# Splitting a mix by head set and key half, and a 64x64-quadrant product with v in three parts, in an attention and feed-forward kernel

## The chip, the core and the metric

The kernel runs on one core of a Trainium2 chip. The metric is the device time of one execution in microseconds (us); lower is better. Names of engines are those of the profile: PE is the matrix engine and PEld its weight loads, DVE, ACT and POOL are the vector, scalar and general engines, SP issues nearly all DMAs.

## What is computed

The reference has two stages, in fp32. The first is attention in which the 12 heads are mixed twice, once before the softmax and once after it; the second is a feed-forward layer with a rational function between its two products.

```python
# q, k, v: (4, 12, 448, 64)
scores = scale * np.matmul(q, k.transpose(0, 1, 3, 2))
scores = np.einsum('bhij,hg->bgij', scores, w_pre)       # first mix
scores = scores - np.max(scores, axis=-1, keepdims=True)
attn = np.exp(scores)
attn = attn / (np.sum(attn, axis=-1, keepdims=True) + 1e-09)
attn = np.einsum('bhij,hg->bgij', attn, w_post)          # second mix
attn_out = np.matmul(attn, v)
...
h = x @ w_in                                             # x: (1792, 768)
P = a[0] + a[1] * h + a[2] * h * h + a[3] * h * h * h
Q = 1.0 + np.abs(b[0]) * np.abs(h) + np.abs(b[1]) * h * h
out = (P / (Q + 1e-6)) @ w_out                           # w_in: (768, 2048)
```

## The kernel before

**Attention.** The 448 query rows of each of the 4 batches are cut into four tiles T of up to 120 rows: 12 tiles have 120 rows, 4 have 88 (computed as 90). For a tile, `put_qk` makes the scores of one head pair at a time (L473, six of them a tile, four matmuls in the four 64x64 quadrants of PE), copies them to SBUF (tile `st`) and sends them by DMA into `d`, where the partitions are (query, head). A *group* is two blocks of 10 queries: six groups in a tile of 120 rows, four and a half in one of 88. `put_pre` does the first mix of a group (L540, four matmuls of 448 columns in the quadrants, into two PSUM banks of pool `ps_t`); DVE takes the row maximum (L547), ACT the exponential with its sum (L556), POOL and DVE the reciprocal, POOL scales the second mix's weights by it (tile `krs`, L576). Two groups later (`LAG`), `put_post` does the second mix (L617): 32 matmuls of 112 columns a group, each in a 64x32 piece of the array, into the two banks of pool `ps_a`. The four 32-row strips of a bank hold the four key quarters, and a block's 224 columns hold the two sets of six heads one behind the other. DVE transposes each bank in 32x32 blocks into `aa` (L633), where keys lie on partitions. When a tile's six groups are transposed, `put_av` multiplies with v (L676): for each half hv of the heads, 24 matmuls of 120 (90) columns, with 128 partitions of contraction, of which 112 carry keys and the rest zeros in v. One half fills one bank of `ps_t`. ACT copies the sum, rounded, to `xs` (L236), DVE writes the rest (L690), and DMAs store both parts to DRAM.

PSUM has eight banks of 128 x 512 words: two in pool `ps_s` (scores), four in `ps_t` (first mix and product with v), two in `ps_a`.

**Feed-forward.** 64 units (`put_unit`): 18 matmuls for h (L832), the rational function on ACT, DVE and POOL, 18 matmuls for the output (L921). Weights come as 64-bit numbers and are converted in pieces by ACT, POOL and DVE (`put_w`, L387 to L431): 16 pieces during attention, to DRAM and back, 48 in the second stage.

**What sets the order.** Nothing is ordered by hand. Each `put_` function adds operations with an engine, an estimated duration, what they depend on and a due time; `Plan.run` plays them through and emits the instructions in that order, engine by engine. On PE the operations of attention are chained (`pe`), each may start only after the one added before it. The duration is also where a mode ("quarters", "eighths", "columns") is named: PE pays `DRAIN` in the plan where the mode changes. Due times follow `tau`, which steps by `SLOT` for a group and `HALF` for half a group. The plan is built once, on the host; on the chip each engine takes its instructions in the given order and waits for what it needs. A `Ring` stands for the buffers of a pool: `take` gives the next, and it is free when the uses of the one n places before are done.

Of the kernel before, what the change touches and what calls it, by code (L numbers as in the profile page):

```python
# [21 lines left out]
G5 = 5  # L22
# [4 lines left out]
TI = 120  # L27
TQ = 128
NT = 4 * B
NJ, JT = 4, 112  # L30
NB, BT = 7, 32
G6 = H // 2
# [209 lines left out]
def mixed_attention_then_rational_ffn(ctx: ExitStack, tc, q, k, v, w, wmix, mask, a, b2, out):  # L242
# [14 lines left out]
          for n, i in (("s", 2), ("t", 4), ("a", 2))}  # L257
# [5 lines left out]
    def open_pools(stack, side, sizes):  # L263
# [9 lines left out]
        ("co", 2), ("ps_s", 2), ("ps_t", 4), ("ps_a", 2), ("a", 2), ("v", 2), ("xs", 1), ("xo", 2),  # L273
# [16 lines left out]
    SLOT, HALF = 3.85, 2.3  # L290
# [233 lines left out]
    def put_pre(g):  # L524
# [54 lines left out]
        slots = [R["ps_t"].take() for _ in range(nt)]  # L579
# [4 lines left out]
        for r in range(nt):  # L584
            o2 = add("dve", dve(S), top(r), [o, free[r]], at=at + 0.5 * r, after=prev[:])
            o3 = add("act", 0.84, exp(r), [o2], at=at + 0.5 * r, after=os[-1:])
            R["ps_t"].uses[slots[r].k].append(o3)
            os.append(o3)
            exps.append(o3)
            prev = [o2]  # L590
# [8 lines left out]
    def put_post(g, at):  # L599
# [37 lines left out]
        o5 = pe(0.95, post, o4 + slots, at, 0.1, "eighths")  # L637
# [12 lines left out]
    def put_v(b, at, gap=8.0):  # L650
        def load(j):
            def fn():
                if j == 0:
                    V[b] = sb["v"].tile([128, NJ, H, D], F32, tag="v", name="vv")
                nc.sync.dma_start(out=V[b][:, j], in_=v[b, :, j])
# [4 lines left out]
        for j in range(NJ):  # L660
            v_ld[b].append(bulk(0.63, load(j), [free] + v_ld[b][:1], at=at + gap * j, nbytes=128 * H * D * 4, since=at + gap * j))

    Xs = {}

    def put_av(T, hv, at):

        b, n, r, c0 = T // 4, rows[T], real[T], row0[T]
        box = {}

        def mm():  # L670
            t = bank("t")
            for pr in range(3):
                for j in range(NJ):
# [7 lines left out]
            box["t"] = t[:, 0:3 * n].rearrange("p (r w) -> p r w", r=3)[:, :, 0:r]  # L681

        def hi(eng):
            if hv == 0 and T % 4 == 0:
                Xs[b] = sb["xs"].tile([128, 2, 2, 3, S], F32R, tag="xs", name="xs")
            move(nc, eng, Xs[b][:, hv, 0, :, c0:c0 + r], box["t"])

        def lo():
            x = Xs[b][:, hv, :, :, c0:c0 + r]
            nc.vector.tensor_sub(x[:, 1], box["t"], x[:, 0].bitcast(F32))  # L690

        def store(hl, cols):
# [3 lines left out]

        slot = R["ps_t"].take()
        o = pe(24 * 0.108 * n / TI, mm, [evac[T], v_ld[b], slot], at, 0.2, "columns")
        av_op[T, hv] = o
        deps, after = [o], []  # L700
        if hv == 0 and T % 4 == 0:
            deps.append(R["xs"].take())
        else:
            after.append(xs_op[b][0])
        h_ = add(copies(3 * n, False, on=ON["x_hi"]), 0, hi, deps, at=at, after=after)
        l_ = add("dve", dve(3 * n), lo, [h_], at=at)
        xs_op.setdefault(b, []).append(h_)
        x_done.setdefault((b, hv), []).append(l_)
        R["ps_t"].uses[slot.k].append(l_)
        R["a"].uses[T].append(o)  # L710
        R["v"].uses[b].append(o)
        if T % 4 > 1:
            last = T % 4 == 3
            cols, done = (slice(c0, S), x_done[b, hv][3:]) if last else (slice(0, c0 + r), x_done[b, hv][:])
            for hl in range(2):
                when = at + (3.0 if last else 5.0) + (1.6 if last else 4.0) * (2 * hl + hv)
                o = bulk(0.45, store(hl, cols), done, at=when, nbytes=128 * 3 * max(cols.stop - cols.start, 240) * 4, late=1.0, since=when - 1.0)
                x_st.setdefault(b, []).append(o)
                R["xs"].uses[b].append(o)
# [12 lines left out]
    for pr in range(H // 2):  # L732
        put_qk(0, pr, at=-8.0 + pr, ps_="stat"[pr % 4])
    early, late = {}, {}
    for T in range(1, NT):
# [4 lines left out]
        for i, pr in zip((2, 3, 4) if T == 1 else (0, 2, 4, 5, 6) if n == 6 else (0, 1, 2, 3, 4), range(ahead, H // 2)):  # L740
            (late if i % 2 else early).setdefault(first[T - 1] + i // 2, []).append((T, pr))
    avs = {}
    for T in range(NT):
        for hv in range(2):
            avs.setdefault(first[T + 1] - 1 + LAG + 1 + hv, []).append((T, hv))
    for g in range(-1, len(groups) + LAG + 3):
# [315 lines left out]
```

## Time and profile before

| what | value |
|---|---|
| runs shown | 877.32, 881.3, 882.75 us (median 881.3) |
| the profiled execution | 876.83 us, of which 875.0 us from its first to its last instruction |
| attention, up to the first matmul of the feed-forward stage | 0 to 392.3 us of the span |
| feed-forward stage | 392.3 to 875.0 us |
| PE busy | 826.2 us, 94% of the span |
| DVE, ACT, POOL busy | 693.0, 483.8, 352.7 us |
| matmul records | 11,088, two for each fp32 matmul of attention |

A busy PE has a matmul somewhere in the array; it is not an array that is full. In attention several matmuls run beside each other in different pieces of the array, so what an operation costs is read from its start to the start of the next one, and not from the duration of its records.

### The profile page before, as it was taken

To read this page: it belongs to the slowest core of one execution; us is meant where nothing else is said; L and a number is where in the kernel's file an instruction comes from. 1 tells how busy PE (TensorE), PEld (TensorE's weight loads), DVE (VectorE), ACT (ScalarE), POOL (GpSimd) and SP (SyncE) were. 2 spreads that over 40 slices of the span, in tenths; PEclk is the share of its full clock that TensorE was granted. 3 is DMA by queue.
4 is the path that set the end of the run, shared out by engine and by line. 5 is a ranking of instruction groups with operands and counts; after the bars stand their busy time and mean duration, and the time that the engine had idled before them with its cause. 6 is when DMAs were issued, how large, how long until landed. Compare 5 with 4: busy or idle time off the path is not lost.

```text
span 875.0 us, 27000 instructions
## 1 busy us (share of the span) xinstructions
PE 826.2 (94%) x11088; PEld 641.3 (73%) x11088; DVE 693.0 (79%) x1279; ACT 483.8 (55%) x1057; POOL 352.7 (40%) x476
## 2 busy tenths in 40 slices
PE   5699989999999899989999999999999999999996
PEld 1255545555555555678898898999999999999995
DVE  5587868797888787847889999999899898666664
ACT  2355656555565554426666566755665567445641
POOL 2234434534344342313545554655555554112111
PEclk9899999999999999999999999999999999999999
DMA  6677788768767863399263337654556653256314
GB/s 204 196 214 216 235 250 239 220 213 283 226 219 232 277 206 117 96 333 372 75 222 121 101 121 265 216 194 138 178 211 208 259 171 126 73 202 231 127 64 147
DMA packets 77548, 170.64 MB, mean 195 GB/s; under 512 B 13072, under 2 KB 54384, under 8 KB 76272
## 3 DMA queue, kind: packets, MB, share of 16 engines
q1 hardware_dynamic: 76824, 167.95, 59.2%
q8 instruction: 87, 1.43, 0.7%
q10 hardware_dynamic: 600, 0.97, 0.3%
q14 instruction: 37, 0.30, 0.1%
HBM read 90.86 MB, written 39.32 MB: 149 GB/s over the span
## 4 chain that ended last, share of the span: by engine, by line
PE 62%; DVE 14%; DMA 5%; issue 4%; ACT 2%; POOL 1%; SPq 0%; DVEq 0%; ACTq 0%; POOLq 0%
PE ps_s L832 19%; PE ps_t L921 13%; PE ps_a L921 7%; PE ps_t L676 7%; PE ps_a L617 6%; PE ps_t L540 5%; PE ps_s L473 5%; DMA d<-st 2%; DVE cg L406 2%; DVE rc L877 1%; DMA x_scr<-xs 1%; DVE cm L412 1%; DVE sq L865 1%; DVE rc L881 1%; DVE sq L874 1%
## 5 line engine op out<-in xcount | busy, mean ns | idle before, releaser
L921 PE MATMUL ps_t<-g,w 128*128 128x448 f32 x768 | 177.4, 366 | 0.9 <-POOL g L891 0.9
L921 PEld LDWEIGHTS ps_t<-g,w 128*128 128x128 f32 x768 | 144.0, 188 | 13.7 <-POOL g L891 1.7
L617 PEld LDWEIGHTS ps_a<-e,krs 64*32 64x32 f32 x5760 | 77.9, 106 | 83.1 <-issue 47.1
L556 ACT ACTIVATE e<-ps_t,nm 128x448 f32<-128x448 f32 x180 | 112.8, 634 | 42.6 <-DVE nm L547 37.1
L891 POOL TENSOR_TENSOR g<-rc,g 128x448 fp32r<-128x448 f32 x55 | 69.1, 1256 | 159.8 <-ACT g L236 88.5
L832 PE MATMUL ps_s<-x,w 128*128 128x448 f32 x576 | 122.5, 366 | 2.1 <-DVE m L861 2.1
L633 DVE STREAM_TRANSPOSE aa<-ps_a 128x448 f32<-128x448 f32 (+1 forms) x184 | 107.8, 618 | 20.8 <-PE ps_a L617 20.1
L832 PE MATMUL ps_s<-xs,w 128*128 128x448 f32 x576 | 122.5, 366 | 1.5 <-DVE m L861 1.5
L397 POOL TENSOR_SCALAR cm<-cm 128x384 f32<-128x384 f32 x64 | 99.5, 1560 | 58.7 <-ACT cm L392 58.6
L617 PE MATMUL ps_a<-e,krs 64*32 64x112 f32 x5760 | 105.5, 263 | 13.1 <-issue 9.5
L832 PEld LDWEIGHTS ps_s<-x,w 128*128 128x128 f32 x576 | 108.0, 188 | 11.7 <-DVE m L861 2.8
L832 PEld LDWEIGHTS ps_s<-xs,w 128*128 128x128 f32 x576 | 107.8, 188 | 11.6 <-DVE m L861 2.6
L473 PE MATMUL ps_s<-kk,q 64*64 64x448 f32 x720 | 98.5, 559 | 15.5 <-DMA q<-in_q 5.3
L547 DVE TENSOR_REDUCE nm<-ps_t 128x1 f32<-128x448 f32 x180 | 104.5, 607 | 7.3 <-PE ps_t L540 6.1
L576 POOL TENSOR_SCALAR krs<-kpost,rr 128x64 f32<-128x64 f32 x180 | 80.3, 461 | 69.5 <-DVE rr L567 55.0
L540 PE MATMUL ps_t<-d,kpre 64*64 64x448 f32 x720 | 93.4, 560 | 7.1 <-DMA x_scr<-xs 2.1
L921 PE MATMUL ps_a<-g,w 128*128 128x448 f32 x384 | 96.5, 366 | 0.0
L236 ACT COPY st<-ps_s 120x448 f32<-120x448 f32 (+1 forms) x101 | 51.3, 533 | 71.8 <-PE ps_s L473 37.3
L676 PE MATMUL ps_t<-aa,vv 128*64 128x120 f32 (+1 forms) x1536 | 84.9, 266 | 0.9 <-DVE aa L633 0.8
L428 POOL TENSOR_TENSOR w<-cm,w 128x384 fp32r<-128x384 f32 x48 | 60.1, 1252 | 57.7 <-ACT w L236 55.8
L845 ACT ACTIVATE m<-ps_s,a_sb 128x448 f32<-128x448 f32 x64 | 46.1, 720 | 67.3 <-PE ps_s L832 67.2
L676 PEld LDWEIGHTS ps_t<-aa,vv 128*64 128x64 f32 x1536 | 77.5, 138 | 6.7 <-issue 5.1
(60 smaller groups left out, 1070.3 us busy)
## 6 DMA issues: line engine op xcount, KB each, us to landing
d<-st SPq DMA_DIRECT2D x144, 210.0 KB
cr<-in_w SPq DMA_DIRECT2D x64, 384.0 KB
o_scr<-o SPq DMA_DIRECT2D x36, 448.0 KB
o<-o_scr SPq DMA_DIRECT2D x36, 448.0 KB
x<-x_scr SPq DMA_DIRECT2D x5, 2688.0 KB
xs<-x_scr SPq DMA_DIRECT2D x4, 2688.0 KB
d<-st SPq DMA_DIRECT2D x42, 157.5 KB
x_scr<-xs SPq DMA_DIRECT2D x12, 540.0 KB
```

Of the source, the lines that this page charges most:

```text
L397: nc.gpsimd.tensor_scalar(out=m, in0=m, scalar1=F64_MIN, scalar2=F64_MAX, op0=ALU.max, op1=ALU.min)
L473: nc.tensor.matmul(box["s"][hh][i0:i1, 0:S], lhsT=Q[T][d, pr, i0:i1], rhs=K[b][d, pr, :], start=True, stop=True)
L540: nc.tensor.matmul(box[r if nt == 2 else 0]["t"][64 * c:64 * c + 64, 0:S], lhsT=kpre[p], rhs=Dt[T][p, kb + c if nt == 2 else kb, :], start ...
L547: nc.vector.tensor_reduce(out=nm, in_=box[r]["t"][:, 0:S], axis=AX.X, op=ALU.max, negate=True)
L556: nc.scalar.activation(e, box[r]["t"][:, 0:S], AF.Exp, bias=box[r]["nm"], accum_out=box[0]["sm"][:, r:r + 1])
L576: eng.tensor_scalar_mul(box[r]["kr"], kpost, rr)
L617: nc.tensor.matmul(banks[c]["p"][BT * q_:BT * (q_ + 1), j0:j0 + JT], lhsT=box[r]["kr"][p, m_, :], rhs=box[r]["e"][p, q_ * JT:(q_ + 1) * JT ...
L633: nc.vector.transpose(o, src)
L676: nc.tensor.matmul(t[64 * hf:64 * hf + 64, pr * n:(pr + 1) * n], lhsT=V[b][:, j, g, :], rhs=A[T][:, 3 * (g // G6) + j, 0:n // G5, G5 * (g ...
L832: nc.tensor.matmul(h[:, 0:S], lhsT=W[fi][:, wi, kk * 128:(kk + 1) * 128], rhs=x[:, kk // 3, xj, kk % 3, :], start=(n == 0), stop=(n == 3 * ...
L891: eng.tensor_sub(g[:, 1, :], box["rc"], g[:, 0, :].bitcast(F32))
L921: nc.tensor.matmul(O[key][:, 0:S], lhsT=W[fi][:, wi, DM + m * 128:DM + (m + 1) * 128], rhs=box["g"][:, gi, :], start=(f == 0 and n == 0), ...
```

## The change

**Second mix.** `put_post` now runs over the two key halves jh and the two head sets m_. A matmul covers 224 keys, so a group has 16 matmuls of 224 columns (32 records) where there were 32 of 112 (64 records). The strips of a bank hold (head set, key half), and its columns are keys alone.

**Product with v.** After the transposes, partitions 0 to 63 hold the first six heads and 64 to 127 the others, with all 448 keys in seven steps of 64 and no padding. v is laid out to match (a batch's four loads of 384 KB become three of 384 KB and one of 192 KB). `put_av` takes a head pair `pr` of each set at a time: 28 matmuls in the four 64x64 quadrants (head set by rows, parity of the head by columns), each head set into a bank of its own. There are three such parts a tile, in three consecutive groups, and the two banks are held over all three; the two evacuations (L236, then L699 in the new numbering) follow the third. The parts carry the mode "quarters", as the scores and the first mix do.

**Banks.** `ps_t` with four banks becomes `ps_t` and `ps_u` with two each. A group's first mix takes a pair. A table made ahead (`pairs`, `holds`) alternates the pairs; while one pair is held by the product with v, the first mixes of these groups all use the other.

**Plan.** `SLOT` goes from 3.85 to 3.65, `HALF` from 2.3 to 2.2, the duration given for the second mix from 0.95 to 0.77.

```diff
-    SLOT, HALF = 3.85, 2.3
+    SLOT, HALF = 3.65, 2.2
...
+        pair = pairs[g]
...
-                box[r]["t"] = bank("t")
+                box[r]["t"] = bank(pair)
...
             for r in range(nt):
-                for m_ in range(2):
-                    for q_ in range(NJ):
+                for jh in range(2):
+                    for m_ in range(2):
                         for c in range(2):
-                            p = slice(64 * c, 64 * c + 64)
-                            j0 = (2 * r + m_) * JT
+                            p, q_ = slice(64 * c, 64 * c + 64), BT * (2 * m_ + jh)
                             nc.tensor.matmul(
-                                banks[c]["p"][BT * q_:BT * (q_ + 1), j0:j0 + JT], lhsT=box[r]["kr"][p, m_, :],
-                                rhs=box[r]["e"][p, q_ * JT:(q_ + 1) * JT], start=True, stop=True)
+                                banks[c]["p"][q_:q_ + BT, JH * r:JH * (r + 1)], lhsT=box[r]["kr"][p, m_, :],
+                                rhs=box[r]["e"][p, JH * jh:JH * (jh + 1)], start=True, stop=True)
...
-        o5 = pe(0.95, post, o4 + slots, at, 0.1, "eighths")
+        o5 = pe(0.77, post, o4 + slots, at, 0.1, "eighths")
...
-    def put_av(T, hv, at):
+    def put_av(T, pr, at):
...
-        box = {}
+        if pr == 0:
+            sums[T] = {}, [R["ps_" + holds[T]].take() for _ in range(2)]
+        box, slots = sums[T]
...
-            t = bank("t")
-            for pr in range(3):
-                for j in range(NJ):
+            if pr == 0:
+                box.update(enumerate([bank(holds[T]), bank(holds[T])]))
+            for j in range(NB):
+                for hv in range(2):
                     for hf in range(2):
-                        g = 2 * (3 * hv + pr) + hf
+                        p, g = slice(64 * hv, 64 * hv + 64), 2 * pr + hf
                         nc.tensor.matmul(
-                            t[64 * hf:64 * hf + 64, pr * n:(pr + 1) * n],
-                            lhsT=V[b][:, j, g, :],
-                            rhs=A[T][:, 3 * (g // G6) + j, 0:n // G5, G5 * (g % G6):G5 * (g % G6 + 1)],
-                            start=(j == 0), stop=(j == NJ - 1))
+                            box[hv][64 * hf:64 * hf + 64, pr * n:(pr + 1) * n], lhsT=V[b][p, j, g, :],
+                            rhs=A[T][p, j, 0:n // G5, G5 * g:G5 * (g + 1)],
+                            start=(j == 0), stop=(j == NB - 1))
...
-        o = pe(24 * 0.108 * n / TI, mm, [evac[T], v_ld[b], slot], at, 0.2, "columns")
+        o = pe(14 * 0.107 * n / TI, mm, [evac[T], v_ld[b]] + (slots if pr == 0 else []), at, 0.2, "quarters")
...
+    pairs, holds, other = {}, {}, {"t": "u", "u": "t"}
+    for g in range(len(groups) + LAG + 4):
+        now, kept = avs.get(g, ()), avs.get(g - 1, ())
+        pairs[g] = pairs[g - 1] if any(pr for _, pr in now) or kept and kept[0][1] == 2 else other[pairs.get(g - 1, "t")]
+        for T, pr in now:
+            if pr == 0:
+                holds[T] = other[pairs[g]]
```

On PE, the stretch of the program in which the product with v of the second tile stands, before. `aa,vv` is the product with v, `e,krs` the second mix, `d,kpre` the first mix, `kk,q` the scores; a row's last figure is the number of matmuls.

```order
L617 MATMUL ps_a<-e,krs 32x112 x32
L676 MATMUL ps_t<-aa,vv 64x120 x24
L473 MATMUL ps_s<-kk,q 64x448 x4
L540 MATMUL ps_t<-d,kpre 64x448 x4
L473 MATMUL ps_s<-kk,q 64x448 x4
L617 MATMUL ps_a<-e,krs 32x112 x32
L676 MATMUL ps_t<-aa,vv 64x120 x24
L540 MATMUL ps_t<-d,kpre 64x448 x4
L617 MATMUL ps_a<-e,krs 32x112 x32
L540 MATMUL ps_t<-d,kpre 64x448 x4
```

The same stretch on PE in the changed kernel; L681 is the product with v, L541 the first mix.

```order
L617 MATMUL ps_a<-e,krs 32x224 x16
L681 MATMUL ps_t<-aa,vv 64x120 x28
L541 MATMUL ps_u<-d,kpre 64x448 x4
L473 MATMUL ps_s<-kk,q 64x448 x4
L617 MATMUL ps_a<-e,krs 32x224 x16
L681 MATMUL ps_t<-aa,vv 64x120 x28
L541 MATMUL ps_u<-d,kpre 64x448 x4
L617 MATMUL ps_a<-e,krs 32x224 x16
L681 MATMUL ps_t<-aa,vv 64x120 x28
L541 MATMUL ps_u<-d,kpre 64x448 x4
L473 MATMUL ps_s<-kk,q 64x448 x4
```

Where two products stood, three stand, each behind a second mix and ahead of a first mix, and the first mixes in between all go to pair `ps_u`, the last two of them with one second mix and one part between.

On DVE, the evacuations of the same tile's products before: one piece each, eight rows apart.

```order
L690 TENSOR_TENSOR xs<-ps_t,xs 128x3x120
L238 COPY st<-ps_s 120x448
L547 TENSOR_REDUCE nm<-ps_t 128x1 x2
L238 COPY st<-ps_s 120x448 x2
L633 STREAM_TRANSPOSE aa<-ps_a 128x2x7x32
L567 RECIPROCAL rr<-sm 128x2
L633 STREAM_TRANSPOSE aa<-ps_a 128x2x7x32
L690 TENSOR_TENSOR xs<-ps_t,xs 128x3x120
```

And on DVE in the changed kernel, such a place.

```order
L633 STREAM_TRANSPOSE aa<-ps_a 128x2x7x32 x2
L568 RECIPROCAL rr<-sm 128x2
L699 TENSOR_TENSOR xs<-ps_t,xs 128x3x120 x2
L548 TENSOR_REDUCE nm<-ps_u 128x1 x2
L238 COPY st<-ps_s 120x448
```

Both evacuations now stand behind the third part, in a row, ahead of the next row maxima.

Over the whole program DVE has 101 copies of scores to `st` (L238) where it had 86, ACT 91 where it had 106. At the end of attention, the last products were 48 matmuls of 90 columns in a row (two halves) and are 84 (three parts), with the feed-forward stage's first matmuls right behind.

## Rows read from the trace of the kernel before

**Rows 1.** The page, part 1: busy time, share of span, instructions.

```profile
PE 826.2 (94%) x11088; PEld 641.3 (73%) x11088; DVE 693.0 (79%) x1279; ACT 483.8 (55%) x1057; POOL 352.7 (40%) x476
```

**Rows 2.** Stages: window, length, busy PE, PEld, DVE, ACT, POOL, clock, DMA, GB/s.

```profile
49.40:372.10 322.70, 305.21 (x7821) 181.82 (x7818) 256.27 (x551) 178.63 (x483) 132.92 (x282) 1.00 0.72 217
392.30:875.00 482.70, 470.49 (x2307) 431.90 (x2304) 397.87 (x655) 284.78 (x525) 203.89 (x151) 1.00 0.51 174
108.00:130.00 22.00, 17.53 (x457) 9.80 (x450) 14.82 (x33) 12.02 (x33) 6.86 (x17) 1.00 0.85 252
262.00:284.00 22.00, 21.96 (x509) 12.47 (x506) 19.64 (x43) 12.41 (x34) 10.87 (x22) 1.00 0.75 230
```

**Rows 3.** What PE waited for, 20 to 392 us: total us, times, longest.

```profile
PE ps_a L617 <- issue: 9.5, 10, 2.0
PE ps_s L473 <- DMA q<-in_q: 5.3, 1, 5.3
PE ps_a L617 <- DVE aa L633: 2.6, 4, 0.8
PE ps_t L540 <- DMA x_scr<-xs: 2.1, 1, 2.1
```

**Rows 4.** PE's timeline, 42 to 60 us: start, length.

```profile
43.49 1.08 PE L617 MATMUL ps_a<-e,krs 64*32 64x112 f32 x64
44.49 0.98 PE L540 MATMUL ps_t<-d,kpre 64*64 64x448 f32 x8
45.30 0.93 PE L473 MATMUL ps_s<-kk,q 64*64 64x448 f32 x8
46.16 0.61 PE L617 MATMUL ps_a<-e,krs 64*32 64x112 f32 x32
46.70 0.98 PE L540 MATMUL ps_t<-d,kpre 64*64 64x448 f32 x8
...
49.37 2.12 PE L676 MATMUL ps_t<-aa,vv 128*64 128x90 f32 x48
51.43 0.98 PE L473 MATMUL ps_s<-kk,q 64*64 64x448 f32 x8
```

**Rows 5.** PE's timeline, 370 to 376 us: a product with v of 120 rows.

```profile
372.05 2.75 PE L676 MATMUL ps_t<-aa,vv 128*64 128x120 f32 x48
374.73 0.98 PE L540 MATMUL ps_t<-d,kpre 64*64 64x448 f32 x8
```

**Rows 6.** Groups by line, whole program: count, busy us, mean ns, idle before.

```profile
L617 PE MATMUL ps_a<-e,krs 64*32 64x112 f32 x5760 | 105.5, 263 | 13.1 <-issue 9.5 <-DVE aa L633 2.6
...
L676 PEld LDWEIGHTS ps_t<-aa,vv 128*64 128x64 f32 x1536 | 77.5, 138 | 6.7 <-issue 5.1 <-DVE aa L633 1.1 <-ACT e L556 0.3
...
L633 DVE STREAM_TRANSPOSE aa<-ps_a 128x448 f32<-128x448 f32 x176 | 105.0, 628 | 18.8 <-PE ps_a L617 18.1
...
L238 DVE COPY st<-ps_s 120x448 f32<-120x448 f32 x63 | 37.8, 616 | 11.4 <-PE ps_s L473 7.5 <-DMA d<-st 3.0 <-PE ps_a L617 0.2
```

**Rows 7.** PE, DVE and ACT timelines, 222 to 226 us: one first mix, its exponentials.

```profile
222.01 0.98 PE L540 MATMUL ps_t<-d,kpre 64*64 64x448 f32 x8
...
223.04 1.16 DVE L547 TENSOR_REDUCE nm<-ps_t 128x1 f32<-128x448 f32 x2
...
224.41 0.62 ACT L556 ACTIVATE e<-ps_t,nm 128x448 f32<-128x448 f32 x1
```

**Rows 8.** ACT, DVE and PE timelines, 386 to 393 us: end of attention.

```profile
390.19 0.38 ACT L236 CAST xs<-ps_t 128x264 fp32r<-128x264 f32 x1 [7.93 <-PE ps_t L676]
...
390.60 0.43 DVE L690 TENSOR_TENSOR xs<-ps_t,xs 128x264 fp32r<-128x264 f32 x1 [3.90 <-ACT xs L236]
...
392.33 0.88 PE L832 MATMUL ps_s<-xs,w 128*128 128x448 f32 x3
```

**Rows 9.** The page, part 3: a DMA queue, its packets, MB, share.

```profile
q8 instruction: 87, 1.43, 0.7%
```

More of the change, by code (lines that the diff above doesn't have):

```diff
@@ L577, in norm @@
             return fn
-        slots = [R["ps_t"].take() for _ in range(nt)]
+        slots = [R["ps_" + pair].take() for _ in range(nt)]
         free = [R["e"].take() for _ in range(nt)]
@@ L659, in put_v @@
         v_ld[b] = []
-        for j in range(NJ):
-            v_ld[b].append(bulk(0.63, load(j), [free] + v_ld[b][:1], at=at + gap * j, nbytes=128 * H * D * 4, since=at + gap * j))
-    Xs = {}
-    def put_av(T, hv, at):
+        for i, j in enumerate(range(0, NB, 2)):
+            v_ld[b].append(bulk(
+                0.63, load(j), [free] + v_ld[b][:1], at=at + gap * i, nbytes=128 * min(2, NB - j) * G6 * D * 4, since=at + gap * i))
+    Xs, sums = {}, {}
+    def put_av(T, pr, at):
         b, n, r, c0 = T // 4, rows[T], real[T], row0[T]
-        box = {}
+        if pr == 0:
+            sums[T] = {}, [R["ps_" + holds[T]].take() for _ in range(2)]
+        box, slots = sums[T]
@@ new lines, in mm, with part, hi, fn @@
+                            rhs=A[T][p, j, 0:n // G5, G5 * g:G5 * (g + 1)],
+                            start=(j == 0), stop=(j == NB - 1))
+        def part(hv):
+            return box[hv][:, 0:3 * n].rearrange("p (r w) -> p r w", r=3)[:, :, 0:r]
+        def hi(hv):
+            def fn(eng):
+                if hv == 0 and T % 4 == 0:
+                    Xs[b] = sb["xs"].tile([128, 2, 2, 3, S], F32R, tag="xs", name="xs")
+                move(nc, eng, Xs[b][:, hv, 0, :, c0:c0 + r], part(hv))
+            return fn
@@ L708, in put_av @@
-        x_done.setdefault((b, hv), []).append(l_)
-        R["ps_t"].uses[slot.k].append(l_)
+        o = pe(14 * 0.107 * n / TI, mm, [evac[T], v_ld[b]] + (slots if pr == 0 else []), at, 0.2, "quarters")
+        av_op[T, pr] = o
         R["a"].uses[T].append(o)
         R["v"].uses[b].append(o)
[L712 to L719, printed above, removed]
+        if pr < 2:
+            return
@@ new lines, in put_av @@
+        for hv in range(2):
+            deps, after = [o], []
+            if hv == 0 and T % 4 == 0:
+                deps.append(R["xs"].take())
+            else:
+                after.append(xs_op[b][0])
+            h_ = add(copies(3 * n, False, on=ON["x_hi"]), 0, hi(hv), deps, at=at, after=after)
+            l_ = add("dve", dve(3 * n), lo(hv), [h_], at=at)
+            xs_op.setdefault(b, []).append(h_)
+            x_done.setdefault((b, hv), []).append(l_)
+            R["ps_" + holds[T]].uses[slots[hv].k].append(l_)
+            if T % 4 > 1:
+                last = T % 4 == 3
+                cols, done = (slice(c0, S), x_done[b, hv][3:]) if last else (slice(0, c0 + r), x_done[b, hv][:])
+                for hl in range(2):
+                    when = at + (3.0 if last else 5.0) + (1.6 if last else 4.0) * (2 * hl + hv)
+                    s_ = bulk(0.45, store(hv, hl, cols), done, at=when, nbytes=128 * 3 * max(cols.stop - cols.start, 240) * 4, late=1.0, since=when - 1.0)
+                    x_st.setdefault(b, []).append(s_)
+                    R["xs"].uses[b].append(s_)
@@ L739, in mixed_attention_then_rational_ffn @@
         n = first[T] - first[T - 1]
-        for i, pr in zip((2, 3, 4) if T == 1 else (0, 2, 4, 5, 6) if n == 6 else (0, 1, 2, 3, 4), range(ahead, H // 2)):
+        for i, pr in zip((2, 3, 4) if T == 1 else (0, 2, 3, 4, 6) if n == 6 else (0, 1, 2, 3, 4), range(ahead, H // 2)):
             (late if i % 2 else early).setdefault(first[T - 1] + i // 2, []).append((T, pr))
@@ L743, in mixed_attention_then_rational_ffn @@
     for T in range(NT):
-        for hv in range(2):
-            avs.setdefault(first[T + 1] - 1 + LAG + 1 + hv, []).append((T, hv))
-    for g in range(-1, len(groups) + LAG + 3):
+        for pr in range(3):
+            avs.setdefault(first[T + 1] + LAG + pr, []).append((T, pr))
+    pairs, holds, other = {}, {}, {"t": "u", "u": "t"}
[5 more added lines that the diff above has]
+                holds[T] = other[pairs[g]]
+    for g in range(-1, len(groups) + LAG + 4):
         if 0 <= g < len(groups):
```

61 lines of the change are left out of this document (22 added, 39 removed).

## The prediction

> **What bounds the kernel now.** I read the busy times by stage first. The reader is to see there two stages that have little in common [rows 2]: attention up to 392.3 us, then the feed-forward stage with 470.5 of 482.7 us of PE busy, which the change does not touch but for names of banks. From 49 to 372 us, attention in steady state, PE is busy 305.2 of 322.7 us, DVE 256.3 (79%), ACT 178.6 (55%), the DMA engines 72%. PE is the fullest, but "busy" says only that some matmul is in the array. So the second view is the list of what PE waited for, which shows how little of attention is a plain wait: 9.5 us on its own issue, 5.3 on one load, 2.6 on the transposes, 2.1 on a DMA [rows 3]. The third is PE's timeline, read from start to start, which gives what each operation holds PE for: second mix 43.49 to 44.49 = 1.00 us, first mix 0.81, scores 0.86 with the change of mode behind them (0.81 and 0.05), a half group's second mix 0.54 [rows 4]; a product with v 2.06 us for 90 columns [rows 4] and 2.68 for 120 [rows 5]. A tile of 120 rows has six of the first three and two products: 6 x 2.67 + 2 x 2.68 = 21.4 us. The first product of the first tile begins at 49.37 [rows 4], that of the fifteenth at 372.05 [rows 5]; the 14 tiles' work between, 11 long and 3 short (4.5 x 2.67 + 2 x 2.06 = 16.1 us), is 284 of the 322.7 us. So attention is for the most part PE's own work, in an order that is fixed, and what an operation gets shorter by moves the end as far as no one else becomes late; the other 39 us are waits spread thin.
>
> **A price for a record.** A fp32 matmul is two records. In a product with v each of the two column halves of the array takes 24 of the 48 records one behind the other, so one holds its half for 2.68/24 = 111.7 ns with 120 columns and 2.06/24 = 85.8 ns with 90. That is 0.861 ns a column and 8.3 ns a record. A test on another shape: the first mix has two records of 448 columns in each quadrant, 2 x (448 x 0.861 + 8.3) = 0.79 us, against 0.81 measured [rows 4]. So four quadrants do work beside each other, and the price carries from halves to quadrants. The second mix does not fit: eight records of 112 columns in each of the eight pieces would be 0.84 us, and it takes 1.00; its 64 records begin every 15.6 ns, which no other operation here comes near.
>
> **Product with v.** It removes two operations of 24 matmuls a tile and adds three of 28. In a quadrant a part has 28 x 2/4 = 14 records. At 111.7 ns that is 1.56 us, three are 4.69 against 5.36: 0.67 us a tile saved, 0.52 with 90 columns. But the old products' times hold two changes of mode each, 0.05 us apiece [rows 4]; the parts have the mode of their neighbours behind them, and what is ahead, the second mix, changes the mode in any case. Without these 0.10 us a record is 107.5 ns (81.7), a part 1.50 us (1.14), and the saving 0.84 us (0.69). With the columns alone, 0.861 ns each, it would be 1.02 (0.87). Twelve tiles of 120 rows and four of 88 give 10.1, 12.8 or 15.7 us. I take 12.8: the mode row is measured, that the 8.3 ns vanish is not.
>
> **Second mix.** 88 full groups lose half of their instructions, with the same columns in all. From below, four records of 224 columns by the price of a record are 0.80 us; from above it stays at 1.00, should the columns and not the instructions be what costs. Nearest is the half group, which already has 32 records: 0.54 us with 112 columns [rows 4]. Each piece of the array has 4 x 112 x 0.861 = 0.39 us of columns more in the new form, so 0.93 us. I take this: 0.07 us x 88 = 6.2 us, between 0 and 17.6. The four half groups stay where they are. The Trainium skill, "TensorEngine Tiling (Array Packing)", section Instruction Overhead, puts about 60 cycles on each matmul, an estimated 25 ns at 2.4 GHz, by which halving 64 records would save 0.8 us a group; the row's 15.6 ns a record lies below such a floor, so I give this no weight.
>
> **Evacuation and end.** The copies and subtractions of the sums are as many as before, but both follow the third part. In the tiles between, they have a first mix, scores and a second mix (2.6 us) before anyone wants their banks, against 1.6 us of work, two of 0.38 and two of 0.43 us [rows 8], and a third more with 120 columns. At the end of attention nothing covers them. Before, the first half went to ACT at 390.19 and was ready at 391.03, under the second half's matmuls, and the feed-forward's first matmul began at 392.33 [rows 8]. Now copy and subtraction of a half, 0.84 us and a hop before it, stand between the last part and that matmul: +1.0 us, 0 to 1.5.
>
> **Held banks.** While a tile's sums hold one pair, four first mixes in a row use the other. Each must find its pair read by both exponentials. From the start of a first mix to the end of its second exponential it takes 225.03 - 222.01 = 3.02 us when DVE is free for it [rows 7]. Three of the four gaps hold scores as well; in the shortest, only a first mix, a second mix and a part stand: 0.81 + 0.93 + 1.50 + 0.05 = 3.29 us. The margin is 0.27 us, once a tile. With one transpose of 0.63 us [rows 6] in front of the row maxima it is overdrawn by 0.36, which would be 5.8 us over 16 tiles. Behind a waiting first mix stands all of PE's queue. I take a quarter, 1.5 us; bounds 0 and 5.8.
>
> **DVE, DMA and loads.** The plan gives DVE 15 copies more, 15 x 0.616 = 9.2 us [rows 6], of which some 8 fall in the steady stretch: (256.3 + 8)/(322.7 - 14) = 86%. From 262 to 284 us DVE already ran at 89% with PE busy all but 0.04 us [rows 2]. I cost it at nothing; without that cover it is up to 9.2 us. Loads of v shrink by an eighth, hidden either way. PE's instructions fall: the second mix has 88 x 32 + 4 x 16 = 2,880 records fewer, the products 16 x 72 = 1,152 more, of 11,088 [rows 1]; each has its weight load. The 9.5 us of PE waiting on issue at the second mix [rows 3] may shrink with them, if the instruction queue of 87 packets [rows 9] feeds PE, which the trace doesn't say. Up to 3 us, not in the sum.
>
> **Sum.** -12.8 - 6.2 + 1.0 + 1.5 = -16.5 us. The profiled execution took 876.83 us (a span of 875.0 and 1.8 around it), so 860.3. It was 4.5 us under the median of the runs shown, 881.3; on that scale the forecast is 865 us. Within 1%, 8.8 us, a measurement of this kernel can hardly tell a change from none.
>
> **Rivals.**
> *The gain is taken by others.* DVE's copies and the short gap are late in most tiles: all of 9.2 and another 4.3 us come back, -3 us, 878. For it speak the 39 us of thin waits, and that from 108 to 130 us, with the DMA engines at 85%, PE was busy for only 17.5 of 22 us [rows 2]; against it the stretch at 262 us.
> *Weight loads show.* In quadrants each part has 56 loads in 1.5 us where a product had 48 in 2.7. If a load can't go under its neighbours' matmuls, each record grows by what the old product's loads hold PEld for, 77.5 us/1536 = 50 ns [rows 6]: a part takes 14 x 157.5 = 2.2 us, 3 x 2.2 against 5.36 is 1.3 us a tile lost (1.4 with 90 columns), +21 us, and with the other terms +17, 899 us. It decides from a part of 1.86 us on. Against it: the price of a record fits the first mix, in quadrants. The Trainium skill, "TensorE: Matmul & The Clock Gate", section Part 3: Packing small matmuls, has the rule behind it: a weight load overlaps matmuls in flight only in another row group. The trace differs in the old product, all of one row group, where 24 records of 120 columns with their loads fit 2.68 us.
> *More than forecast.* The second mix falls to 0.80 us (11.4 us more) or the waits on issue shrink: 850 to 857.
> *It doesn't do what it says.* Two banks instead of four, or the shuffles into `d`, set the pace, and PE only waits longer: 878 to 882.
>
> **How the numbers follow.** Forecast, 857 to 872: 0.70. More: 0.08. Gain taken, 872 to 880: 0.15. Loads show, near 899: 0.05. No effect: 0.02. Faster by over 1% are the first two and a little of the third: 0.79; slower the fourth and a remnant: 0.06; the rest 0.15. The range leaves out the fourth and the edges: 856 to 878.
>
> **What would show it.** In the new profile, start to start on PE: a part at 1.45 to 1.56 us for 120 columns, a second mix at 0.93, first mixes and scores unchanged at 0.81; a gap ahead of the feed-forward's first matmul of about 1 us; PE's first mix waiting for exponentials for no more than a few us in all; the feed-forward stage as long as before. I am wrong if a part takes over 1.86 us, if DVE's idle time is gone while PE's waits grow, or if the second mix stays at 1.00.

## The result and the profile after

| | before | after |
|---|---|---|
| median of the first comparison | 882.02 us (4 runs) | 867.71 us (4 runs) |
| ratio, 95% interval | | 0.9875 (0.9843 to 0.9907) |
| median of the later repeat | 880.78 us (35 runs) | 873.8 us (12 runs) |
| ratio in the repeat, 95% interval | | 0.9933 (0.9899 to 0.9967) |
| profiled execution | 876.83 us | 867.26 us |
| first matmul of the feed-forward stage | 392.33 us | 382.44 us |

The change makes the kernel faster, by 1.25% in the first comparison and 0.7% in the repeat. The forecast was 865 us; the medians are 867.7 and 873.8. All of it lies in attention: the feed-forward stage takes 483.1 us where it took 482.7 [rows 2].

The page, part 1, and its instruction queue, which answer to [rows 1, 9]:

```profile
PE 814.4 (94%) x9360; PEld 604.9 (70%) x9360; DVE 702.2 (81%) x1288; ACT 478.9 (55%) x1044; POOL 359.5 (42%) x480
...
q8 instruction: 74, 1.21, 0.6%
```

Two stages, columns as in [rows 2]: from the first part of the first tile's product to that of the fifteenth's, and the feed-forward stage.

```profile
46.30:362.80 316.50, 293.74 (x6234) 149.12 (x6226) 267.47 (x570) 168.00 (x459) 133.81 (x280) 0.99 0.73 220
382.40:865.50 483.10, 471.45 (x2308) 431.66 (x2304) 393.22 (x639) 288.35 (x529) 205.74 (x153) 1.00 0.51 175
```

The steady stretch is 316.5 us long where it was 322.7. The forecast for it was 308.7 us. PE has 11.5 us less to do in it and DVE 11.2 us more, so DVE went from 79% to 85% (forecast 86%).

PE's timeline around one tile's product of 120 rows, and the first part of a tile of 88, which answer to [rows 4, 5]:

```profile
191.67 0.99 PE L617 MATMUL ps_a<-e,krs 64*32 64x224 f32 x32
192.59 1.70 PE L681 MATMUL ps_u<-aa,vv 64*64 64x120 f32 x56
194.12 0.92 PE L541 MATMUL ps_t<-d,kpre 64*64 64x448 f32 x8
195.01 1.43 PE L617 MATMUL ps_a<-e,krs 64*32 64x224 f32 x32
196.36 1.70 PE L681 MATMUL ps_u<-aa,vv 64*64 64x120 f32 x56
197.85 0.53 PE L541 MATMUL ps_t<-d,kpre 64*64 64x448 f32 x1
...
212.21 1.34 PE L681 MATMUL ps_u<-aa,vv 64*64 64x90 f32 x56
213.36 0.93 PE L541 MATMUL ps_t<-d,kpre 64*64 64x448 f32 x8
```

Start to start, the second mix takes 0.92 us (191.67 to 192.59; forecast 0.93, before 1.00). A part takes 1.53 and 1.49 us here (forecast 1.50) and 1.15 with 90 columns (forecast 1.14). The prices of the operations came as worked out.

What PE waited for from 20 us to the feed-forward stage, which answers to [rows 3]:

```profile
PE ps_s L473 <- DMA q<-in_q: 6.3, 3, 3.5
PE ps_a L617 <- issue: 4.0, 3, 1.7
PE ps_u L541 <- DVE st L238: 3.7, 2, 3.0
PE ps_u L681 <- issue: 3.3, 3, 1.9
PE ps_t L541 <- DMA d<-st: 3.1, 2, 1.6
PE ps_s L473 <- DVE st L238: 2.6, 5, 1.0
PE ps_u L541 <- DMA d<-st: 2.5, 2, 1.9
PE ps_t L541 <- issue: 2.4, 1, 2.4
```

Waits on issue stand at the second mix still, and now at the parts too. The first mix (L541) waits for shuffles into `d` and for the copies ahead of them; of its 3.7 us for copies, 3.0 are one wait that began at 17.45 us and ended at 20.47, where the first tile's mixes begin. PE never waits there for an exponential: the held pair of banks costs nothing that this view shows. (The weight loads of the first mix wait 1.7 us for exponentials in the same stretch, 4.9 in the kernel before.)

The end of attention, PE's timeline, then ACT's, which answer to [rows 8]:

```profile
375.27 4.99 PE L681 MATMUL ps_u<-aa,vv 64*64 64x90 f32 x164 [0.84 <-DVE aa L633]
382.13 0.38 PE L681 MATMUL ps_u<-aa,vv 64*64 64x90 f32 x4 [1.88 <-issue]
382.44 11.57 PE L851 MATMUL ps_s<-xs,w 128*128 128x448 f32 x54
```

```profile
380.31 0.38 ACT L236 CAST xs<-ps_u 128x264 fp32r<-128x264 f32 x1 [7.80 <-PE ps_u L681]
382.56 0.38 ACT L236 CAST xs<-ps_u 128x264 fp32r<-128x264 f32 x1 [1.87 <-PE ps_u L681]
```

The feed-forward stage starts at 382.44, before the second sum is even copied (382.56). The gap of 0.84 us that I had put ahead of it is not there. PE waits 1.88 us on issue with four records of the last part to go, and the first sum is copied meanwhile (380.31). Where PE doesn't stand so late in the last part, the copy of the first sum shows: in the run with 32 matmuls of 112 and the one with earlier scores, both below, the first feed-forward matmul waits 0.36 and 0.48 us for it.

**Where the gain went.** The sum of all rows of the view of waits, taken off the time from 20 us to the feed-forward stage, leaves the work. A wait that began before 20 us counts from 20 us on; each of these kernels has one, ahead of the first mixes of the first tile. Waits inside an operation and a lower clock count as work in this. Each row of the table is worked out so, from one profiled execution (the number of waits on issue in brackets; the kernels of the lower rows come below):

| kernel | feed-forward starts | waits | on issue | on DMA | on others | work |
|---|---|---|---|---|---|---|
| before | 392.33 | 26.3 | 9.7 (11) | 9.6 | 7.1 | 346.0 |
| after | 382.44 | 30.6 | 9.7 (7) | 12.5 | 8.4 | 331.9 |
| after, again | 382.19 | 32.5 | 9.4 (7) | 14.6 | 8.5 | 329.7 |
| before, less DMA | 376.52 | 14.3 | 2.0 (4) | 6.8 | 5.5 | 342.3 |
| after, less DMA | 370.61 | 22.6 | 8.9 (7) | 6.6 | 7.1 | 328.0 |
| 32 matmuls of 112 | 417.00 | 46.0 | 28.1 (28) | 7.9 | 10.0 | 351.0 |
| the same, less DMA | 401.13 | 35.1 | 26.5 (25) | 4.2 | 4.4 | 346.0 |

PE's work shrank by 14.1 and 16.3 us; the two terms of the forecast for it, 12.8 and 6.2, are 19.0. Waits grew by 4.3 and 6.2 us and took three to four tenths of it back: 2.9 and 5.0 us of that are waits on DMA, 1.3 and 1.4 on others, and none at full load is on issue.

### The profile page after: what moved, and what is told of

Read it like the earlier page. It is cut to its first block, busy times and chain, and to the rows that moved or that the text cites. A ratio compares the mean times of both kernels' runs of the same rounds, so it can differ in the third digit from the quotient of the medians.

```text
span 865.5 us, 23553 instructions
## 1 busy us (share of the span) xinstructions
PE 814.4 (94%) x9360; PEld 604.9 (70%) x9360; DVE 702.2 (81%) x1288; ACT 478.9 (55%) x1044; POOL 359.5 (42%) x480
## 3 DMA queue, kind: packets, MB, share of 16 engines
q8 instruction: 74, 1.21, 0.6%
## 4 chain that ended last, share of the span: by engine, by line
PE 61%; DVE 19%; DMA 9%; issue 6%; ACT 4%; SPq 0%; POOL 0%; DVEq 0%; ACTq 0%; POOLq 0%
PE ps_s L851 15%; PE ps_a L617 8%; PE ps_s L473 7%; DMA d<-st 6%; PE ps_u L940 5%; PE ps_t L940 5%; PE ps_a L940 5%; PE ps_u L541 4%; PE ps_t L541 4%; PE ps_u L681 4%; PE ps_t L681 3%; DVE sq L893 2%; DVE rc L900 2%; DVE m L880 2%; DVE o L977 2%
## 5 line engine op out<-in xcount | busy, mean ns | idle before, releaser
L633 DVE STREAM_TRANSPOSE aa<-ps_a 128x448 f32<-128x448 f32 (+1 forms) x184 | 108.0, 617 | 13.4 <-PE ps_a L617 12.8
L473 PE MATMUL ps_s<-kk,q 64*64 64x448 f32 x720 | 102.6, 558 | 14.1 <-DMA q<-in_q 6.3
L617 PEld LDWEIGHTS ps_a<-e,krs 64*32 64x32 f32 x2880 | 46.4, 107 | 83.3 <-issue 34.7
L617 PE MATMUL ps_a<-e,krs 64*32 64x224 f32 x2880 | 97.7, 360 | 6.6 <-issue 4.0
L940 PE MATMUL ps_u<-g,w 128*128 128x448 f32 x384 | 96.2, 365 | 0.0
L940 PE MATMUL ps_t<-g,w 128*128 128x448 f32 x384 | 96.0, 365 | 0.0
L557 ACT ACTIVATE e<-ps_t,nm 128x448 f32<-128x448 f32 x92 | 57.7, 634 | 45.0 <-DVE nm L548 39.2
L564 POOL TENSOR_SCALAR sm<-sm 128x2 f32<-128x2 f32 (+1 forms) x92 | 23.1, 251 | 137.3 <-ACT e L557 135.6
L236 ACT COPY st<-ps_s 120x448 f32<-120x448 f32 (+1 forms) x83 | 42.4, 533 | 67.9 <-PE ps_s L473 45.7
L557 ACT ACTIVATE e<-ps_u,nm 128x448 f32<-128x448 f32 x88 | 55.2, 634 | 38.9 <-DVE nm L548 35.5
L473 PEld LDWEIGHTS ps_s<-kk,q 64*64 64x64 f32 x720 | 31.7, 134 | 64.2 <-issue 23.7
L940 PEld LDWEIGHTS ps_u<-g,w 128*128 128x128 f32 x384 | 72.1, 188 | 6.1
```

Source lines behind the costliest of these rows:

```text
L473: nc.tensor.matmul(box["s"][hh][i0:i1, 0:S], lhsT=Q[T][d, pr, i0:i1], rhs=K[b][d, pr, :], start=True, stop=True)
L557: nc.scalar.activation(e, box[r]["t"][:, 0:S], AF.Exp, bias=box[r]["nm"], accum_out=box[0]["sm"][:, r:r + 1])
L617: nc.tensor.matmul(banks[c]["p"][q_:q_ + BT, JH * r:JH * (r + 1)], lhsT=box[r]["kr"][p, m_, :], rhs=box[r]["e"][p, JH * jh:JH * (jh + 1)], ...
L633: nc.vector.transpose(o, src)
L940: nc.tensor.matmul(O[key][:, 0:S], lhsT=W[fi][:, wi, DM + m * 128:DM + (m + 1) * 128], rhs=box["g"][:, gi, :], start=(f == 0 and n == 0), ...
```

## The experiments

Two theories at first. **The instruction stream**: PE's instructions come in a queue of their own, the parts stand in a denser stretch than the old products did, and PE waits for instructions. **The other engines and the DMAs**: DVE, with more copies, or the transfers that the shorter order asks for sooner, are late. For the second, the copies were also more than the forecast said: DVE has 97 copies from `ps_s` where it had 79, and one more from the other banks. That is 105 where it had 86 (not 101, as I had counted), so 19 more and not 15.

**The number of instructions.** The second mix in its new layout, but with each matmul cut in two:

```diff
-                for jh in range(2):
-                    for m_ in range(2):
+                for x in range(0, JH, JH // 2):
+                  for jh in range(2):
+                    for m_ in range(2):
...
-                                banks[c]["p"][q_:q_ + BT, JH * r:JH * (r + 1)], lhsT=box[r]["kr"][p, m_, :],
-                                rhs=box[r]["e"][p, JH * jh:JH * (jh + 1)], start=True, stop=True)
+                                banks[c]["p"][q_:q_ + BT, JH * r + x:JH * r + x + JH // 2], ...
+                                rhs=box[r]["e"][p, JH * jh + x:JH * jh + x + JH // 2], ...)
```

> The changed kernel with each matmul of 224 columns of the second mix cut into two of 112, so 32 matmuls a group again, into the new layout; all else the same. If PE's own work sets the pace of attention, 88 groups x 0.08 us come back: about +7 us on the changed kernel's 867.7, so 873 to 876, and a second mix takes 1.00 us from start to start. If DMAs or DVE set it, less than half of that shows: 867 to 871.

901.18 us, ratio 1.0207 (1.0164 to 1.0251): the product with v in quadrants is then a loss. PE's waits, its record rate over the product of one tile, and its instruction queue:

```profile
PE ps_a L618 <- issue: 11.1, 14, 2.8
PE ps_u L682 <- issue: 9.9, 8, 3.1
PE ps_t L541 <- issue: 4.7, 3, 2.7
```

```profile
205.25:216.19 10.94, 10.73 (x383) 1.00 0.82 254
```

```profile
q8 instruction: 96, 1.57, 0.7%
```

The feed-forward stage starts 34.6 us later than in the changed kernel. The second mix costs 1.01 us again, 88 x 0.09 = 7.9 us. Waits on issue are 28.1 where they were 9.7, 18.4 us more, the others 3.0 less. For the remaining 11 there is an estimate only: the stage's granted clock is 0.96 and not 0.98, which over 397 us would be about 8. The stretch shown holds 383 records in 10.94 us, 35 a microsecond; the changed kernel's like stretch, 191.67 to 201.99 us, has 287 in 10.32 (28), and the kernel before, 194.51 to 204.00, 245 in 9.49 (26). So halving the number of matmuls is worth not 6.2 us beside these parts, but some 27 to 35 (901.2 us against medians of 873.8 and 867.7, and 34.6 us by the stage's start).

**Less DMA.** k and v of batch 0 are loaded once and used for all batches, so that three quarters of these loads are left out: 8.3 MB by the traces in the changed kernel, 8.9 in the one before. The edit is the same in both but for the form of v's loads; the changed kernel's is shown:

```diff
-                    K[b] = sb["k"].tile([128, H // 2, S], F32, tag="k", name="kk")
-                nc.sync.dma_start(out=K[b][:, i * n:(i + 1) * n], in_=k[b, :, i * n:(i + 1) * n])
+                    K[b] = K[0] if b else sb["k"].tile([128, H // 2, S], F32, tag="k", name="kk")
+                if b == 0:
+                    nc.sync.dma_start(out=K[b][:, i * n:(i + 1) * n], in_=k[b, :, i * n:(i + 1) * n])
...
+                    V[b] = V[0] if b else sb["v"].tile(...)
```

> The changed kernel, in which batches 1 to 3 use k and v of batch 0, so that 8.1 of some 80 MB of attention's DMA traffic is not moved; the order of all other instructions is the same, the output is that of other data. If DMAs took back the missing 5 us (waits for q and for the shuffles into d), 859 to 864, and these waits shrink. If DVE took it, 866 to 869.

> The kernel before, in which batches 1 to 3 use k and v of batch 0 (8.5 MB less DMA traffic in attention, output of other data), the same cut as made on the changed kernel, where it gave 11 us. If the changed kernel fell short because its shorter operations ran into the DMAs, the kernel before gains clearly less than 11 us from the same cut: 1 to 5 us, ratio 0.994 to 1.0. If DMAs held both back alike, it gains 8 to 12 us too, ratio near 0.987, and the shortfall has another cause.

856.76 us (ratio 0.9721, 0.968 to 0.9762) for the changed kernel, 862.22 us (0.9844, 0.9772 to 0.9916) for the one before. The kernel before gains 16.5 us, more than the 8 to 12 expected, and the changed one 11 to 17. DMA holds both up alike as far as these intervals tell, so it isn't what the change in particular ran into. The pair shows more: with less DMA the feed-forward stage starts only 5.9 us sooner than in the kernel before, while the work is 14.3 us less. Of the 8.3 us of waits that come in between, 6.9 are on issue (2.0 against 8.9), although the program has 1,728 matmul records fewer. But 1.4 of the 8.9 are the wait that ends at 21.40 us, ahead of the first mixes of the first tile; the other profiles name a copy or a shuffle there. Without it, 7.5 us in 6 waits are left.

The same instructions wait in each execution of these parts. PE's timeline of the changed kernel, of its repeat, and with less DMA, at the third part of the first tile and at the last part of attention (shown for the first above, 382.13):

```profile
55.33 0.79 PE L681 MATMUL ps_u<-aa,vv 64*64 64x90 f32 x27 [0.74 <-issue]
```

```profile
57.71 0.79 PE L681 MATMUL ps_u<-aa,vv 64*64 64x90 f32 x27 [2.34 <-issue]
...
381.70 0.56 PE L681 MATMUL ps_u<-aa,vv 64*64 64x90 f32 x4 [3.37 <-issue]
```

```profile
57.78 0.79 PE L683 MATMUL ps_u<-aa,vv 64*64 64x90 f32 x27 [2.62 <-issue]
...
370.39 0.29 PE L683 MATMUL ps_u<-aa,vv 64*64 64x90 f32 x1 [2.71 <-issue]
```

With 27 records of the third part in one row, and 4 or 1 of the last part to go, PE stands still for 0.7 to 3.4 us. Data can hardly be late there: the parts ahead have read the same loads of v, and the transposes are waited for ahead of a part.

The DMA packets in the traces show what PE waits for. The instruction queue `q8` moves packets of 16,384 bytes, one for some 127 records of PE. Ahead of each of the three waits at the last part, one of them starts; the DMA view from 379.20 to 380.00 us in the changed kernel, 378.80 to 379.60 in its repeat, 367.50 to 368.20 with less DMA:

```profile
q8 instruction: 1, 0.02, 7.2%
```

```profile
q8 instruction: 1, 0.02, 7.2%
```

```profile
q8 instruction: 1, 0.02, 9.9%
```

The seven profiles of the table have 89 waits on issue from 20 us to the feed-forward stage. 85 of them end 2.2 to 2.9 us after the start of such a packet (of the 113 other waits, 13 do), and within one program these 85 stand a whole number of blocks of 125 to 128 records apart. The other four are 0.2, 0.2 and 0.7 us long, and the one at 21.40 us. So PE stands at the edge of a block of instructions until the next block is there. The place belongs to the program; how long PE stands there differs between executions.

**Both edits at once.**

> Two edits at once: the second mix's matmuls cut into halves of 112 columns (32 a group again, as in the earlier run), and k and v of batch 0 loaded once and used for all batches (8.1 MB less DMA; the output is then not the reference's). Theory A, the waits on instructions need DMA queues under load, since instructions come by DMA: 862 to 872 us, not more than 15 us over the run with less DMA alone (856.8). Theory B, the number of instructions a microsecond suffices by itself: 880 to 890 us, 25 to 33 us over it, as with the full DMA load.

885.03 us, ratio 1.005 (1.0013 to 1.0086), 28.3 us over the run with less DMA alone: theory B. Waits on issue are 26.5 us, as with the full load:

```profile
PE ps_a L619 <- issue: 11.4, 12, 2.5
PE ps_u L684 <- issue: 7.0, 5, 2.9
```

So with this many instructions PE waits for them however busy the DMA engines are with data. In the kernel before the load did count (9.7 against 2.0), in the changed kernel a little (9.7 and 9.4 against 7.5).

**DVE.** The conversion of the 16 weight pieces that falls in attention is left out on DVE (the three steps of `put_w` return at once for them); DVE then has 17.6 us less to do from 20 to 382 us (280.3 against 297.9), not the 30 expected.

```diff
+            if f < PH:
+                return
```

> The changed kernel without the three DVE steps of the 16 weight pieces that are converted during attention (30 us of DVE's time left out, DMAs, ACT and POOL as they are; these weights come out wrong). If DVE's load took back the missing 5 us, 859 to 864. If DMAs did, 866 to 869.

869.5 us, ratio 0.9867 (0.9821 to 0.9913); the feed-forward stage starts at 382.55 us. Nothing is gained, and the theory of DVE falls. The other way round, the first head of each pair is always copied by ACT (57 copies of 120 rows on DVE for 76):

```diff
-            c = add(copies(S, False, on=ON["s"]), 0, copy(hh), [o, R["st"].take()], at=at)
+            c = add(copies(S, False, on=("act",) if hh == 0 else ON["s"]), 0, copy(hh), ...)
```

> The changed kernel with the copy of each pair's first head fixed to ACT, which gives DVE 77 copies of scores where it has 105 (17 us of DVE less in attention), ACT 115 for 87. If DVE's load is the price, 862 to 866; if DMAs are, 866 to 869; if ACT becomes late with its in-order queue, 870 and more.

878.78 us, ratio 0.9985 (0.9946 to 1.0025): no gain over the kernel before can be told. The feed-forward stage starts 7.0 us later than in the changed kernel, and the scores wait 7.1 us for ACT, which they didn't there:

```profile
PE ps_s L473 <- ACT st L236: 7.1, 9, 1.3
```

**Loads, buffers and the plan's step.** Three edits against the waits on DMA: q due 8 us sooner; eight `st` buffers for six; `SLOT` and `HALF` back to the values before.

```diff
-        put_q(T, at=tau[first[T - 1]] - (13.0 if T > 2 else 9.0) if T > 1 else 1.0, ...)
+        put_q(T, at=tau[first[T - 1]] - (21.0 if T > 2 else 9.0) if T > 1 else 1.0, ...)
```

> The changed kernel with the loads of q due, and allowed, 8 us earlier from the fourth tile on; nothing else is changed, but the plan makes its order anew. If the time of these loads is what counts, the 6.3 us of PE waiting for q go, 861 to 865. If it is the sum of the traffic in the loaded stretches, the wait moves to the shuffles into d, 866 to 870.

873.13 us (865.82 to 880.58), ratio 0.991 (0.9866 to 0.9954), feed-forward from 382.40. The median is above both expectations, and not to be told from the repeat's 873.8. The waits for q fall from 6.3 to 1.5 us; in their place PE waits 4.4 us for a load of v.

```diff
-    open_pools(right, "right", (("st", 6), ("q", 3), ("k", 2)))
+    open_pools(right, "right", (("st", 8), ("q", 3), ("k", 2)))
```

> The changed kernel with eight buffers for copied scores in place of six. In the changed kernel DVE waits 10 us in front of these copies for a buffer that a shuffle has not left yet, with all of DVE's queue behind. If that is how late DMAs reach PE, 861 to 865; if the shuffles are late in any case, 866 to 870.

867.24 us (864.14 to 873.36), ratio 0.9891 (0.9854 to 0.9927), feed-forward from 385.60: no difference that can be told.

```diff
-    SLOT, HALF = 3.65, 2.2
+    SLOT, HALF = 3.85, 2.3
```

> The changed kernel with the plan's steps as before, SLOT 3.85 and HALF 2.3; the estimates of the operations stay. If due times matter only as an order, 866 to 869. If the earlier due times of loads and weight pieces crowd the DMA queue, 861 to 865; if the longer steps now hold back loads that are wanted earlier, 870 to 878.

873.69 us (867.64 to 876.43), ratio 0.9938 (0.9898 to 0.9977), feed-forward from 390.31 in the profiled execution. The new step may be worth a few us, but the interval reaches over the changed kernel's.

**The order of scores and parts.** The changed kernel once more, then two other orders of the same work.

> The changed kernel once more, unaltered. All theories: 864 to 871 us, a ratio of 0.984 to 0.991 to the kernel before; the first feed-forward matmul at 381 to 385 us of the span. If the waits of PE on issue fall at the same blocks of the program as in its first profile, they belong to the order of the instructions; if they fall elsewhere, to chance on the DMA queues.

873.8 us (866.63 to 878.58), ratio 0.9933 (0.9899 to 0.9967), above what I expected; the feed-forward stage starts at 382.19 all the same. Its waits on issue are 9.4 us in 7 places for 9.7 in 7, and those at the parts stand where they stood.

```diff
-        for i, pr in zip((2, 3, 4) if T == 1 else (0, 2, 3, 4, 6) if n == 6 else (0, 1, 2, 3, 4), ...):
+        for i, pr in zip((2, 3, 4) if T == 1 else (0, 1, 2, 3, 4) if n == 6 else (0, 1, 2, 3, 4), ...):
```

> The fifth head pair's scores of a tile stand a group earlier (places 0 to 4 for every tile, not 0, 2, 3, 4 and 6), so that the shuffles of the next tile can land before its first mix. Work is the same. If shuffles that land late are what took part of the gain: the waits of the first mix on them (5.6 us in the changed kernel) go and the time is 861 to 865 us. Rival: the scores then wait for their loads or for free buffers instead, 866 to 873 us.

877.32 us, ratio 0.9962 (0.9924 to 1.0), feed-forward from 389.81. The first mixes wait 2.4 us for shuffles, all of it ahead of the first tile's (21.85 us), where it was 5.6 (13.6 in the repeat), and PE's waits in all fall to 25.6 us; yet the end is later, above both expectations. Weight loads of the scores waited for the copies that free their two banks, from 20 us on in this kernel:

```profile
PEld ps_s L473 <- ACT st L236: 26.0, 45, 1.8
...
PEld ps_s L473 <- DVE st L238: 22.8, 45, 2.2
```

and in the changed kernel:

```profile
PEld ps_s L473 <- ACT st L236: 14.6, 33, 0.8
PEld ps_s L473 <- DVE st L238: 14.2, 25, 1.8
```

Such waits inside an operation don't show as PE's idle time, since its other matmuls run on; they count as work (344.2 us by the table's rule, 12.3 more than in the changed kernel). I read them so: five groups in a row with scores are more than the two banks of `ps_s` bear.

```diff
-            avs.setdefault(first[T + 1] + LAG + pr, []).append((T, pr))
+            avs.setdefault(first[T + 1] + LAG, []).append((T, pr))
...
-        pairs[g] = pairs[g - 1] if any(pr for _, pr in now) or kept and kept[0][1] == 2 else ...
+        pairs[g] = pairs[g - 1] if any(pr for _, pr in now) or kept and kept[-1][1] == 2 else ...
```

> The three parts of a tile stand in a row, 84 matmuls, behind one second mix, instead of one part behind each of three. Work and instructions are the same, and the pair of banks is held over one gap instead of three. Theory of the instruction stream: a denser burst (32 and 168 records in a row) empties PE's instruction queue, waits on issue grow and the time is 872 to 882 us. Rival, the held banks: the short gaps with one pair cost the missing time; with fewer of them 860 to 866 us and waits on issue as before.

888.09 us, ratio 1.0072 (1.0035 to 1.0109), slower than both expected. Waits on issue don't grow (7.2 us), so the theory of the instruction stream is wrong about this order: 84 matmuls in a row did not cost more of them; and with the pair held for one gap only nothing is won, which speaks against the rival too. Of its waits, the largest are:

```profile
PE ps_t L541 <- DMA d<-st: 4.9, 1, 4.9
PE ps_u L541 <- DVE st L238: 4.4, 1, 4.4
PE ps_t L541 <- DMA x_scr<-xs: 4.3, 3, 2.5
```

The granted clock of the stage is 0.96, not 0.98. The work was not the same after all: planned anew, ACT has 112 copies of scores and DVE 80, where the changed kernel has 87 and 105. That is nearly the split of the run with the first heads on ACT (115 and 77), which was slower too. So whether the order or the copies on ACT made the copies and shuffles late stays open, and neither theory is settled by this run.

## Why the prediction was nearly right

**Product with v, -12.8.** Right by price: parts of 1.49 to 1.53 and 1.15 us. The mode's 0.05 us and the 8.3 ns a record, taken from the old product, carried over to quadrants. The rival of the weight loads, which decided from 1.86 us a part, is out.

**Second mix, -6.2.** Right by price, 0.92 us for 0.93; wrong in what it is worth. Its instructions are halved just where the parts bring more of them, and with the old number the change as a whole is 2% slower than the kernel before. By the estimate from the Trainium skill that I had given no weight ("TensorEngine Tiling (Array Packing)", section Instruction Overhead), the group itself would have become 0.8 us cheaper; it became 0.08 cheaper.

**Held banks, +1.5.** Not there: in no gap does a first mix of PE wait for an exponential. In one of the shortest gaps the second mix takes 1.35 us (195.01 to 196.36), 0.43 over its price, for another reason (in another, at 121.49, it waits 0.58 us for a reciprocal and takes 1.42). PEld's timeline at 195 us:

```profile
194.97 0.14 PEld L617 LDWEIGHTS ps_a<-e,krs 64*32 64x32 f32 x2 [0.71 <-POOL krs L577]
195.44 0.56 PEld L617 LDWEIGHTS ps_a<-e,krs 64*32 64x32 f32 x30 [0.33 <-DVE aa L633]
```

It waits for the transposes to empty the `ps_a` bank of the mix before, which came only 3.3 us earlier. Six rows of that length (1.39 to 1.43 us) stand in attention, 6 x 0.43 = 2.6 us in all. The other five stand where no pair is held, three of them near the end where no scores are left, so this is no price of the held pair; that the total lies within the bounds 0 to 5.8 is chance.

**End of attention, +1.0.** Too large: the first feed-forward matmuls don't need the last sum, only the copy of the first (0.36 and 0.48 us in two other runs). In both profiles of the changed kernel that copy is hidden under the wait on issue, 1.9 and 3.4 us.

**DVE at no cost.** Right, by the run without its conversions.

**Waits on issue, 0 to -3, not in the sum.** I let fewer instructions mean less of such waits, and that was wrong. They are fewer, 7 for 11, but longer: at full load 9.4 to 9.7 us as before, and with less DMA 7.5 where the kernel before has 2.0. What goes with them between these kernels is how dense a stretch is, 26 records a microsecond before and 28 after, 35 in the run at 901 us; that density is what counts is not shown, and the run with 84 matmuls in a row doesn't bear it out.

**The sum.** -16.5 us was forecast, -9.6 was profiled. The step that failed is that what an operation gets shorter by moves the end, with waits of others at +1.0 and +1.5 only, loads hidden and DVE at nothing. The work fell by 14.1 and 16.3 us instead of 19.0, and no row shows where the other 3 to 5 stayed. Waits grew by 4.3 and 6.2 us: at full load through DMA for the most part, with less DMA through instructions. The account that fits, argued and not shown, is that every other supplier of PE (shuffles, loads, instructions) is asked sooner, by 10 us at the stage's end. That was the rival "taken by others", in a size between its 878 and the forecast, but not through DVE's load. That the median came within 3 us of 865 is in part luck: the medians of the first comparison lie 14.3 us apart, those of the repeat 7.0.

**Left open.** Which waits come back differs from run to run (DMA 12.5 and 14.6 us in two profiles of the same kernel). That PE waits for packets of the instruction queue is shown by their times; why a block comes late at one edge and not at another is not, and no run delays that queue alone. Of the versions tried, none is clearly faster than the changed kernel.

## What to carry to other kernels

A price read from start to start held for the operation and carried to other shapes here, but the sum of such prices is more than the gain: three to six tenths of the work saved came back as waits of an engine that was already 94% busy. Where work is cut into more and smaller matmuls, count the instructions of a stretch as well as of the program, and look at the waits on issue there: whether they stand a fixed number of instructions apart, and what the instruction queue moves just ahead of them. A second edit that looks like a small gain in time can be what makes the first one pay, if it takes instructions out of the same stretch.

## What was unexpected of the hardware

The queue `q8 instruction` grows with PE's records: 1.43 MB for 11,088 [rows 1, 9], 1.21 for 9,360, 1.57 for 12,240, that is 128 to 129 bytes for a matmul with its weight load, in packets of 16 KB. The Trainium skill ("Runtime: NRT & Kernel Launch", section Instruction fetch mechanics) has an engine's instructions fetched in blocks of that size, at a cost that is mostly hidden. The trace agrees on the block, and mostly on the cost: the changed kernel's profile has 7 waits, of up to 2.4 us (3.4 in its repeat), for the 52 blocks from its first such wait to its last; the run with 12,240 records has 27 for 72.

A wait of PE can cost twice. After 3.53 us without a matmul, scores ran at half the clock; PE's timeline, and the window behind it with the granted clock third from the right:

```profile
128.93 1.60 PE L473 MATMUL ps_s<-kk,q 64*64 64x448 f32 x8 [3.53 <-DMA q<-in_q]
```

```profile
129.20:132.60 3.40, 3.00 (x40) 0.66 (x32) 0.31 (x1) 2.05 (x6) 0.99 (x1) 0.50 0.89 250
```

Scores took 1.52 us there (to 130.45), against 0.86 [rows 4]. That is 1.2 GHz for 2.4. A wait for instructions did the same: after the 2.41 us on issue that ended at 223.40, the clock was 0.50 from 224.75 to 228.14, and the second mix in it took 1.67 us for 0.92.
